# Two token tiles' queries in one projection, by halves of the features

## The chip, the cores and the metric

The kernel runs on one core of one Trainium2 chip. The core has five engines with their own instruction queues: TensorE (matmuls, results go to PSUM), VectorE, ScalarE, GpSimd, and SyncE, which here only issues DMA transfers. Each queue is worked off in its own order, and the engines wait for one another through semaphores. The metric is the device time of one execution in microseconds.

## The reference

Two kinds of layer, A and B, are applied in turn, A B A B, to a residual stream x of 2048 tokens by 512 features. Each adds its result to x after a layer norm. There are 32 heads of 16 features.

```python
x = x + _A_ref(_layernorm(x, axis=-1), A_wq, A_wk, A_wv, A_wo, A_beta)
x = x + _B_ref(_layernorm(x, axis=-1), B_wqkv, B_w_phi, B_wo)
x = x + _A_ref(_layernorm(x, axis=-1), A_wq, A_wk, A_wv, A_wo, A_beta)
x = x + _B_ref(_layernorm(x, axis=-1), B_wqkv, B_w_phi, B_wo)
```

Layer A works on 4 segments of 512 tokens. Within a segment it is causal attention; beside it a memory M, z of the earlier segments is read with phi of the queries and added with a gate.

```python
phi = lambda t: jnp.where(t > 0, t + 1.0, jnp.exp(t))
for s in range(N):
    logits = jnp.einsum('bhqd,bhkd->bhqk', qs, ks) * scale + mask
    p = _softmax(logits, axis=-1)
    a_dot = jnp.einsum('bhqk,bhkd->bhqd', p, vs)
    pq = phi(qs)
    num = jnp.einsum('bhld,bhde->bhle', pq, M)
    den = jnp.einsum('bhld,bhd->bhl', pq, z)[..., None] + 1e-06
    o = g * (num / den) + (1.0 - g) * a_dot
    pk = phi(ks)
    M = M + jnp.einsum('bhld,bhle->bhde', pk, vs)
    z = z + jnp.einsum('bhld->bhd', pk)
```

Layer B is linear attention over all 2048 tokens with softmax features of q and k. The change touches layer A alone, and within it the queries.

## The kernel before

The residual stream X stays in SBUF as 16 token tiles of 128. A segment of layer A, and a chunk of layer B, is four token tiles.

**Layer A's projections** (`a_proj`). The normalized rows of a segment come transposed into `xA`, features on the partitions. For each token tile the kernel projects keys, queries and values. The queries come out with features on the partitions: `fm_mms` makes 16 matmuls for one token tile, four groups g of 128 features by four slices dt of the contraction, each with a 128 x 128 block of `WA_q` as the weights and the tile's 128 tokens as the moving columns. The 16 fill one PSUM bank of 512 columns, ordered by group and then by token. One copy (`q.copy`, on ScalarE or VectorE) takes the bank to `QT`, a buffer for two token tiles (4 groups x 256 tokens), into the tile's 128 columns of each group. In segments 1 to 3 phi of the queries follows, one token tile at a time: an exponential on ScalarE (`phiq.exp`, L944) from `QT` into the buffer `phi`, max(q + 1, 1) on VectorE (`phiq.lin`, L945) into `PhiQ`, and the smaller of the two on VectorE (`phiq.min`, L946). In segment 0 the memory is empty and no phi of the queries is needed. The first two token tiles of segment 0 are projected in a direct form (`by_pe`), with their transposes on TensorE. Keys and values (`WA_k`, `WA_v`) go by `proj_heads`, with tokens on the partitions and 256 columns to a matmul. Keys are then transposed by DMA (`kT.dma`).

**Scores** (`a_att`). A segment has 18 pairs of score tiles, each a PE operation of 8 to 28 matmuls of 32 contraction rows over `QT` and `K`, and two exponentials of 128 x 1024 on ScalarE (L1089) into `PT`. The diagonal blocks are masked on GpSimd and VectorE (L1095, L1098). The products with the values follow on TensorE (rows `PS<-VT,PT` and `PS<-VT,D`), then a reciprocal and a normalization on VectorE (L1123, L1124). A score operation waits for the parts of `QT` that it reads; a part is one token tile.

**The memory read** (`a_mem`) waits for `PhiQ`, and its parts are token tiles too.

**The order of the work** is written out. The program first makes a list of some 3,400 operations, each with the engines that can do it. `replay` then puts them into the queues in the order of the table `ORDER`; `ENGINE` has a letter for each operation that more than one engine can do; `SLOTS` chooses the buffer of each tile; `AFTER` adds waits of one operation for another. A negative entry of ORDER stands for idle matmuls: -1 - 16 n - b puts n matmuls of 240 columns into a corner of PSUM bank b, whose results nobody reads (L1417). The waits themselves follow from what each operation reads and writes.

**The loads** (`setup`, `late_loads`) of X and of the weights stand in the queues of SyncE and ScalarE among the DMA transposes, in the places that ORDER gives them. X comes as four tiles of 128 rows and three loads of 512 rows (segments 1 to 3); VectorE takes statistics of these rows (`stats`, L786) in `ln`.

Of the kernel before, what the change touches and what calls it, by code (L numbers as in the profile page):

```python
# [7 lines left out]
ACT = mybir.ActivationFunctionType  # L8
# [516 lines left out]
class Kernel:  # L525
# [134 lines left out]
    def gen(self):  # L660
        return self.PS.tile(self.genkind)
# [213 lines left out]
    def a_proj(self, s, xnT, pris, by_pe=()):  # L875

        self.P.tag = (self.L, "aproj%d" % s)
        R, P = self.R, self.P
        K, VT = self.p_K.tile(), self.p_VT.tile()
        seg = dict(K=K, VT=VT, KP=[self.p_KP.tile() for _ in range(4)], QT=[self.p_QT.tile() for _ in range(2)])  # L880
        if s >= 1:
            seg["PhiQ"] = self.p_PhiQ.tile()
        if s <= 2:
# [578 lines left out]
```

## Time and profile before

| | before |
|---|---|
| median of 3 runs | 451.51 us |
| lowest, highest | 451.43, 451.68 us |
| the profiled execution's own time | 453.82 us |
| its span, first to last instruction | 452.0 us |
| TensorE busy | 435.1 us (96%) |
| VectorE busy | 417.2 us (92%) |
| ScalarE busy | 412.0 us (91%) |
| GpSimd busy | 258.0 us (57%) |
| mean granted TensorE clock | 0.992 |

PE is TensorE's matmuls, PEld its weight loads, DVE VectorE, ACT ScalarE, POOL GpSimd, SP SyncE. A busy TensorE counts each matmul to the modelled end of its result, so it isn't TensorE at its peak. A row of the timeline has the start, the time, the engine, the line and the operation, out<-in with the shapes, the number of instructions, and in brackets how long the engine was idle before it and what ended that. A row of the windows has a stretch, its length, and for each engine the busy time and the number of instructions; PEclk is the granted clock as a share of full speed, then come the DMA engines' share and GB/s. A row of the groups has the total busy time and the mean in ns, and then the idle time before.

### The profile page before, as it was taken

The numbers are of one execution on the slowest core, as the hardware profiler recorded it, in microseconds if no ns is written. First come the engines' busy times: TensorE is split into PE (matmuls) and PEld (weight loads), VectorE is DVE, ScalarE is ACT, GpSimd is POOL, SyncE is SP. The second block draws the span as 40 slices with busy tenths as digits, with TensorE's granted clock in tenths as the row PEclk, the third lists the DMA queues.
The fourth block names the chain that finished last, engine by engine and source line by source line (L and its number), as shares of the span: only waits on it lengthen the run. The fifth ranks groups of instructions, "written<-read, shape, count | busy, mean of one in ns | idle before, by whom it ended". The sixth has DMA issues, their size and how long they took to land.

```text
span 452.0 us, 19039 instructions
## 1 busy us (share of the span) xinstructions
PE 435.1 (96%) x8236; PEld 303.9 (67%) x8236; DVE 417.2 (92%) x1043; ACT 412.0 (91%) x633; POOL 258.0 (57%) x429
## 2 busy tenths in 40 slices
PE   7979999999999999999999999999999999999996
PEld 6775767667766665757777666876676765675763
DVE  7978999989999899899999999999998989968996
ACT  4989999999999999897899999999999999999730
POOL 4557578675775587330157677766786677814100
PEclk9998999989999999999999999999999999999999
DMA  8986773516213320522525647256134224032377
GB/s 246 235 131 119 107 143 38 85 35 96 50 27 38 62 39 13 74 46 48 74 56 87 96 64 105 49 86 83 27 38 83 49 51 49 3 73 51 76 132 210
DMA packets 115092, 35.86 MB, mean 79 GB/s; under 512 B 106816, under 2 KB 115008, under 8 KB 115008
## 3 DMA queue, kind: packets, MB, share of 16 engines
q1 hardware_dynamic: 112464, 32.41, 42.3%
q10 hardware_dynamic: 2544, 2.24, 1.7%
q8 instruction: 65, 1.06, 1.0%
q14 instruction: 19, 0.16, 0.1%
HBM read 6.32 MB, written 2.10 MB: 19 GB/s over the span
## 4 chain that ended last, share of the span: by engine, by line
ACT 51%; PE 34%; DVE 9%; DMA 3%; issue 1%; SPq 1%; DVEq 0%
ACT PT L1089 38%; PE PS L505 33%; ACT Ek L1185 5%; DMA X<-in_A_x_dram 3%; ACT phi L944 2%; ACT K L1268 2%; ACT phi L933 1%; DVE Vt L1213 1%; PE PS L586 1%; DVE stats L786 1%; ACT VT L564 1%; DVE KV L1240 1%; DVE Rkv L1242 1%; DVE X L1150 1%; DVE PT L1324 1%
## 5 line engine op out<-in xcount | busy, mean ns | idle before, releaser
L1089 ACT ACTIVATE PT<-PS 128x1024 bf16<-128x1024 f32 x288 | 281.6, 1099 | 5.6 <-PE PS L505 4.8
L1098 POOL TENSOR_SCALAR_AFFINE_SELECT PT<-PT 128x512 bf16<-128x512 bf16 x128 | 80.9, 640 | 45.5 <-DVE D L1095 32.5
L1095 POOL TENSOR_TENSOR D<-PT,modd 128x256 bf16<-128x256 bf16 x118 | 77.7, 670 | 36.3 <-ACT PT L1089 10.3
L505 PEld LDWEIGHTS PS<-VT,PT 128*128 128x128 bf16 x2048 | 74.3, 96 | 16.6 <-DVE O L1124 2.0
L505 PE MATMUL PS<-VT,PT 128*128 128x17 bf16 x2048 | 80.5, 171 | 2.3 <-DVE O L1124 1.6
L505 PE MATMUL PS<-VT,D 128*128 128x17 bf16 x512 | 60.0, 171 | 0.0
L505 PE MATMUL PS<-QT,K 32*128 32x64 bf16 (+2 forms) x2176 | 56.3, 214 | 3.8 <-ACT PT L1089 2.4
L786 DVE BATCH_NORM_STATS2 stats<-X 128x6 f32<-128x512 bf16 x64 | 42.5, 677 | 4.2 <-DMA X<-in_A_x_dram 3.9
L1150 DVE TENSOR_TENSOR X<-X,PS 128x512 bf16<-128x512 bf16 x64 | 42.9, 679 | 3.1 <-PE PS L505 2.9
L505 PEld LDWEIGHTS PS<-QT,K 32*128 32x128 bf16 x2176 | 29.5, 93 | 22.0 <-ACT PT L1089 14.5
L505 PEld LDWEIGHTS PS<-VT,D 128*128 128x128 bf16 x512 | 43.2, 96 | 0.0
L1095 DVE TENSOR_TENSOR D<-PT,modd 128x256 bf16<-128x256 bf16 x138 | 38.2, 302 | 3.5 <-ACT PT L1089 3.0
L1213 DVE TENSOR_TENSOR Vt<-PS,Zk 128x1024 bf16<-128x1024 f32 (+1 forms) x34 | 38.8, 1154 | 1.2 <-PE PS L505 0.6
L1185 ACT ACTIVATE Ek<-PS 128x512 bf16<-128x512 f32 x64 | 38.2, 683 | 1.3 <-PE PS L505 1.3
L505 PE MATMUL PS<-xA,WA_q 128*128 128x128 bf16 x512 | 36.3, 224 | 0.3 <-ACT K L906 0.2
L505 PE MATMUL PS<-WA_v,xA 128*128 128x256 bf16 x256 | 35.6, 276 | 0.0
L505 PE MATMUL PS<-WA_k,xA 128*128 128x256 bf16 x256 | 34.6, 273 | 0.3
L1288 POOL COPY O<-rho 128x512 bf16<-128x512 bf16 x26 | 15.7, 622 | 33.4 <-DVE rho L1281 11.3
L1192 POOL TENSOR_TENSOR Vt<-Ek 128x512 f32<-128x512 bf16 x24 | 27.7, 1156 | 10.6 <-ACT Ek L1185 4.8
L505 PEld LDWEIGHTS PS<-xA,WA_q 128*128 128x128 bf16 x512 | 30.7, 100 | 4.4 <-issue 1.3
L505 PE MATMUL PS<-WA_o,OT 128*128 128x512 bf16 x128 | 33.0, 380 | 0.0
L1124 DVE TENSOR_TENSOR O<-PS,r 128x256 bf16<-128x256 f32 (+1 forms) x72 | 27.4, 384 | 1.1
(162 smaller groups left out, 936.0 us busy)
## 6 DMA issues: line engine op xcount, KB each, us to landing
X<-in_A_x_dram SPq DMA_DIRECT2D x3, 512.0 KB, 8.2
out_dram<-X ACTq DMA_DIRECT2D x9, 128.0 KB, 2.1
EQ<-in_B_wqkv_dram SPq DMA_DIRECT2D x2, 512.0 KB, 7.1
out_dram<-X SPq DMA_DIRECT2D x7, 128.0 KB, 2.3
OT<-O SPq DMA_TRANSPOSE x36, 3.3
WA_o<-in_A_wo_dram SPq DMA_DIRECT2D x1, 512.0 KB, 10.7
WB_v<-in_B_wqkv_dram SPq DMA_DIRECT2D x1, 512.0 KB, 6.3
WB_o<-in_B_wo_dram SPq DMA_DIRECT2D x1, 512.0 KB, 5.4
```

The costliest lines, as they stand in the source:

```text
L505: return e.matmul(o, l, r, start=st, stop=sp, tile_position=(basep(l), basep(o)))
L786: self.dve(lambda e, t=t, src=src: e.bn_stats(self.stats[:, t, :], src()), 0.603, [held() if held else R("X", t)], [R("stats", t)], name=" ...
L944: self.act(lambda e, t3=t3, src=src: e.activation(t3.ap[:].rearrange("p (g c) -> p g c", g=NG), src(), ACT.Exp), 512, [sres], [t3()], name ...
L1089: self.act(lambda e, st=st, pt=pt: e.activation(pt.ap[:].rearrange("p b c -> p (b c)"), self.ps[:, st.slot[0] * 512:st.slot[0] * 512 + 102 ...
L1095: self.either(lambda e, d=d, k=k, pt=pt: e.tensor_tensor(d.ap[:, :, k, :].rearrange("p b (z c) -> p b z c", z=2), self.ends(pt.ap[:, :, 25 ...
L1098: self.pool(lambda e, q=quarters: e.affine_select(q(), q(), [[0, 4], [1, 128]], ALU.is_ge, 0.0, base=0, channel_multiplier=-1), 0.6, [pt() ...
L1124: self.dve(lambda e, r1=r1, view=view, nt=nt, g=g, o=o[ts]: e.tensor_tensor(o.ap[:, 0:nt, g, :].rearrange("p i (h d) -> p i h d", d=DH), v ...
L1150: self.dve(lambda e: e.tensor_tensor(X[:, t, :], X[:, t, :], self.bank(gen), ALU.add), 0.6, [R("X", t), gen()], [R("X", t)], name="resid")
L1185: self.act(lambda e, sgn=sgn, Ek=Ek, gen=gen: e.activation(Ek.ap[:, sgn, :], self.bank(gen), ACT.Exp, scale=1.0 - 2.0 * sgn), 512, [gen()] ...
L1192: self.pool(lambda e, Ek=Ek, sums=sums: e.tensor_tensor(sums(), *(Ek.ap[:].rearrange("p s (h j) -> p s h j", h=H)[:, :, :, 8 * k:8 * k + 8 ...
L1213: self.dve(lambda e, w=w, n=n, Vt=Vt, Zk=Zk, gen2=gen2: e.tensor_tensor(self.signed(Vt)[:, w, :, 0:16], self.bank(gen2).rearrange("p (h d) ...
L1288: P.add(("act", "pool"), {"act": lambda e, dst=dst, src=src: e.activation(dst(), src(), ACT.Copy), "pool": lambda e, dst=dst, src=src: e.t ...
```

## The change

The queries of token tiles 0 and 1, and of 2 and 3, of a segment are projected together, when the odd one is reached. There are two halves h of the features: for each half 8 matmuls (two groups by four slices) of 256 columns, both token tiles at once, into a bank of their own, and a copy of the bank into the half's groups of `QT`. A part of `QT` is now a half of the features for both token tiles; so are the parts of `PhiQ`, the exponential, the linear piece and the minimum. `phiq.lin` can go to VectorE or GpSimd; 11 of 24 are given to VectorE and 13 to GpSimd. The direct tiles of segment 0 stay as they were. `seg["q"]` holds for each token tile the two resources that a score has to wait for, and a score now takes that of its group's half.

Of the 512 matmuls with `WA_q`, 448 of 128 columns give way to 224 of 256. The number of operations is unchanged, and all of them outside the queries keep their number in ORDER. ORDER, ENGINE, SLOTS and AFTER are all new. ORDER has 16 entries of idle matmuls in place of 14, with 79 matmuls in place of 76; AFTER has 171 waits in place of 178. Of the tables the core shows only lines of the new ORDER with idle matmuls in them (-39 and -34: two each; -71: four).

```diff
@@ -31,181 +31,182 @@
...
+    191, 363, 724, 364, 211, 232, 216, 217, 196, 233, 237, 175, 214, -39, 201, 15, 202, 203, 204, 726, 205, 215, 365, 428, 176, 341, 218, 219, -34,
...
+    777, 650, 479, 663, 622, 651, 662, 625, 480, 623, 656, 624, 660, 682, 626, -34, 667, 668, 684, 785, 683, 627, 489, 673, 674, 678, 1116, 669, 814,
+    670, -71, 685, 686, 747, 687, 786, 676, 490, 671, 675, 672, 482, 483, 816, 677, 679, 680, 815, 484, 817, 493, 706, 708, 494, 688, 681, 689, 818,
...
@@ -877,7 +878,7 @@
         self.P.tag = (self.L, "aproj%d" % s)
         R, P = self.R, self.P
         K, VT = self.p_K.tile(), self.p_VT.tile()
-        seg = dict(K=K, VT=VT, KP=[self.p_KP.tile() for _ in range(4)], QT=[self.p_QT.tile() for _ in range(2)])
+        seg = dict(K=K, VT=VT, KP=[self.p_KP.tile() for _ in range(4)], QT=[self.p_QT.tile() for _ in range(2)], q={})
         if s >= 1:
             seg["PhiQ"] = self.p_PhiQ.tile()
         if s <= 2:
@@ -933,17 +934,31 @@
                     self.act(lambda e, t2=t2, src=src: e.activation(heads(t2.ap[:]), src(), ACT.Exp), 512, [gen()], [t2()], name="phik.exp")
                     self.dve(lambda e, kt=kt, dst=dst: e.tensor_scalar(heads(dst()), self.spread(kt), 1.0, 1.0, op0=ALU.add, op1=ALU.max), 0.21, [kt()], [res], port=True, name="phik.lin")
                     self.dve(lambda e, t2=t2, dst=dst: e.tensor_tensor(dst(), dst(), t2.ap[:], ALU.min), 0.334, [res, t2()], [res], port=True, name="phik.min")
-            qt, qs = seg["QT"][tt // 2], slice((tt % 2) * 128, (tt % 2) * 128 + 128)
-            t3 = self.p_phi.tile() if s >= 1 else None
-            gen = self.gen()
-            P.pri = pris[tt]
-            self.steps(self.fm_mms(W["q"], xnT, tt, gen), self.wa("q") + [xnT(tt)], gen, pre=[qt] + ([t3] if s >= 1 else []), n=8, name="q")
-            self.copy(lambda qt=qt, qs=qs: qt.ap[:, :, qs], lambda gen=gen: self.bank(gen).rearrange("p (g c) -> p g c", g=NG), 512, [gen()], [qt(tt % 2)], name="q.copy")
-            if s >= 1:
-                dst, res, src, sres = (lambda sl=sl: seg["PhiQ"].ap[:, :, sl]), seg["PhiQ"](tt), (lambda qt=qt, qs=qs: qt.ap[:, :, qs]), qt(tt % 2)
-                self.act(lambda e, t3=t3, src=src: e.activation(t3.ap[:].rearrange("p (g c) -> p g c", g=NG), src(), ACT.Exp), 512, [sres], [t3()], name="phiq.exp", cost=0.52)
-                self.dve(lambda e, dst=dst, src=src: e.tensor_scalar(dst(), src(), 1.0, 1.0, op0=ALU.add, op1=ALU.max), 0.21, [sres], [res], port=True, name="phiq.lin")
-                self.dve(lambda e, t3=t3, dst=dst: e.tensor_tensor(dst(), dst(), t3.ap[:].rearrange("p (g c) -> p g c", g=NG), ALU.min), 0.334, [res, t3()], [res], port=True, name="phiq.min")
+            if direct:
+                qt, qs = seg["QT"][tt // 2], slice((tt % 2) * 128, (tt % 2) * 128 + 128)
+                gen = self.gen()
+                P.pri = pris[tt]
+                self.steps(self.fm_mms(W["q"], xnT, tt, gen), self.wa("q") + [xnT(tt)], gen, pre=[qt], n=8, name="q")
+                self.copy(lambda qt=qt, qs=qs: qt.ap[:, :, qs], lambda gen=gen: self.bank(gen).rearrange("p (g c) -> p g c", g=NG), 512, [gen()], [qt(tt % 2)], name="q.copy")
+                seg["q"][tt] = [qt(tt % 2)] * 2
+            elif tt % 2:
+                qt, sl = seg["QT"][tt // 2], slice((tt - 1) * 128, (tt + 1) * 128)
+                P.pri = pris[tt - 1]
+                for h in range(2):
+                    t3 = self.p_phi.tile() if s >= 1 else None
+                    gen = self.gen()
+                    mms = [(lambda g=g, dt=dt, h=h, gen=gen, tt=tt: (self.bank(gen)[:, (g - 2 * h) * 256:(g - 2 * h + 1) * 256], W["q"][:, dt, g * 128:(g + 1) * 128],
+                                                                     self.xtiles(xnT)[:, tt - 1:tt + 1, dt, 0:128], dt == 0, dt == 3), 256) for g in (2 * h, 2 * h + 1) for dt in range(4)]
+                    self.steps(mms, self.wa("q") + [xnT(tt - 1), xnT(tt)], gen, pre=[qt] + ([t3] if s >= 1 else []), n=4, name="q")
+                    self.copy(lambda qt=qt, h=h: qt.ap[:, 2 * h:2 * h + 2, :].rearrange("p g c -> p (g c)"), lambda gen=gen: self.bank(gen), 512, [gen()], [qt(("g", h))], name="q.copy")
+                    for i in (tt - 1, tt):
+                        seg["q"].setdefault(i, []).append(qt(("g", h)))
+                    if s >= 1:
+                        dst, res, src, sres = (lambda sl=sl, h=h: seg["PhiQ"].ap[:, 2 * h:2 * h + 2, sl]), seg["PhiQ"]((tt // 2, h)), (lambda qt=qt, h=h: qt.ap[:, 2 * h:2 * h + 2, :]), qt(("g", h))
+                        two = lambda t3=t3: t3.ap[:].rearrange("p (g c) -> p g c", g=2)
+                        self.act(lambda e, t3=t3, src=src, two=two: e.activation(two(), src(), ACT.Exp), 512, [sres], [t3()], name="phiq.exp", cost=0.48)
+                        self.either(lambda e, dst=dst, src=src: e.tensor_scalar(dst(), src(), 1.0, 1.0, op0=ALU.add, op1=ALU.max), 0.21, 0.6, [sres], [res], name="phiq.lin")
+                        self.dve(lambda e, two=two, dst=dst: e.tensor_tensor(dst(), dst(), two(), ALU.min), 0.334, [res, t3()], [res], port=True, name="phiq.min")
             P.pri = pris[tt] + (2.0 if by_pe else 0.0)
             gen = self.proj_heads(W["v"], self.wa("v"), xnT, tt, pre=[VT], name="v")
             self.copy(lambda tt=tt: VT.ap[:, tt, :, 0:16].rearrange("p (a b) d -> p b a d", b=2), lambda gen=gen: halves(gen), 512, [gen()], [VT(tt)], name="v.copy")
@@ -983,14 +998,14 @@
         AM, r2 = self.p_AM.tile(), self.p_r2.tile()
         gen = self.gen()
         self.pe([(lambda i=i, g=g: (self.bank(gen)[:, i * 32 + 8 * g:i * 32 + 8 * g + 8], PhiQ.ap[:, g, i * 128:(i + 1) * 128], MSb.ap[:, g, :, 16], True, True), 8)
-                 for i in range(4) for g in range(NG)], [PhiQ(i) for i in range(4)] + [MSb(1)], [gen()], pre=[r2], name="den")
+                 for i in range(4) for g in range(NG)], [PhiQ((t, h)) for t in range(2) for h in range(2)] + [MSb(1)], [gen()], pre=[r2], name="den")
         dst = lambda: r2.ap[:].rearrange("p i h -> p (i h)")
         self.dve(lambda e: e.tensor_scalar(dst(), self.bank(gen, 128), DEN_EPS, None, op0=ALU.add), 0.21, [gen()], [r2()], name="den.eps")
         self.dve(lambda e: e.reciprocal(dst(), dst()), 0.87, [r2()], [r2()], name="den.rec")
         for i in range(4):
             g2 = self.gen()
             self.pe([(lambda g=g, i=i, g2=g2: (self.bank(g2)[:, g * 128:(g + 1) * 128], PhiQ.ap[:, g, i * 128:(i + 1) * 128], MSb.ap[:, g, :, 0:16], True, True), 128)
-                     for g in range(NG)], [PhiQ(i), MSb(0), r2()], [g2()], pre=[AM], name="am")
+                     for g in range(NG)], [PhiQ((i // 2, h)) for h in range(2)] + [MSb(0), r2()], [g2()], pre=[AM], name="am")
             self.dve(lambda e, i=i, g2=g2: e.tensor_tensor(AM.ap[:, i, :].rearrange("p (h d) -> p h d", h=H), self.bank(g2).rearrange("p (h d) -> p h d", h=H),
                                                      r2.ap[:, i, :, None].to_broadcast([128, H, DH]), ALU.mult), 0.6, [g2(), r2()], [AM(i)], name="am.mul")
         return AM
@@ -1075,11 +1090,11 @@
                 g = item[1]
                 if item[0] == "S":
                     par, j, qs = item[2:]
-                    reads += [K((par, j)), K((par, j, 1)), K(("both", j))] + [QT[i // 2](i % 2) for i in qs]
+                    reads += [K((par, j)), K((par, j, 1)), K(("both", j))] + [seg["q"][i][g // 2] for i in qs]
                     put(lambda a, par=par, g=g, j=j: strip(a, par, g, j), item, qs[0] * 128, off, 128 * len(qs))
                 else:
                     i = item[2]
-                    reads += [K((1, i)), K((0, i)), K((1, i, 1)), K(("both", i)), seg["KP"][i](), QT[i // 2](i % 2)]
+                    reads += [K((1, i)), K((0, i)), K((1, i, 1)), K(("both", i)), seg["KP"][i](), seg["q"][i][g // 2]]
                     put(lambda a, g=g, i=i: both(a, g, i), item, i * 128, off, 64)
                     for par in range(2):
                         put(lambda a, par=par, g=g, i=i: strip(a, par, g, i), item, i * 128 + 64, 6 + off // 4 if par else off + 1, 64)
```

More of the change, by code (lines that the diff above doesn't have):

```diff
@@ L33 @@
 ORDER = (
[135 rows of a table removed]
[135 rows of a table added]
 )
 AFTER = (
[17 rows of a table removed]
[17 rows of a table added]
 )
 ENGINE = (
[L190 to L193 removed]
+    "aaddaadapaapaddpadpdpdpadddapdpdppdddpdddddddpppppppppddddddpdddpdpapapdpdpaddpdpdpdaddddadadppppppppppdppppppdddddddddddppdpppppdddddddddpa"
@@ L194 @@
+    "dddapdddpdpdddddddpdppdpppppdddddpppdddddpppddppppddppdpppdpdpddddpdddpdddpddddaddddddddppddppppdddpdddpddddpddpddpddpddpdddppppddddddaappap"
+    "apppaaaaaaaddaaapaapdaapaadadaadddaapppdppddppddpddpddpdpddpddpdppdddapdpadapapadadapdpddapdapppppppdppppppppdddddpddddpdpdpppppdppppdddpapd"
+    "aadapdddpdpaaapaddpaddppppppddppppdddddddpddddpppddddpdppppppdddddpapddddaddddpdddpdddpdpdppppppddddddddddppddddddppppdppdddpddpdddpdddaapap"
+    "aappasaaasassssaasasasda"
 )
 SLOTS = (
-    "00030010120110132260011103001801000001202301111210320045011217910320011231210231010121381000002231041000313211356100223010113079011212200370"
@@ L205 @@
-    "10100021530211471012032106120010351000213212011001121304801001110379011102332211301002001302901220157011013280231123013121049012130214010110"
-    "10003510201972100532012002210100141031100310225601020123801011023201030002101220120012140110133750100000112223369011131201300130131482102100"
-    "01206012202501000122207901130202010110102323010213001451020002010147015010202230007003120110024531112260010220033106112403101202001313101213"
-    "451549310411036102378203442050157"
+    "00110010020101301800112103010312012203210690111310102033410110057102011030022160122130002139201022318010103120341000011213057013021222093021"
@@ new lines @@
+    "12701452030210820101102031031013210201179011300201121004012000025210100220301102201701133101015201114612030001120820013901010303002170112110"
+    "00304610210231032350110020290113010130102031003110315010017821203010129201211003512012002000810120311792012001121201000000310500113021340102"
+    "13680210021010203311150101012210210100100134301322167100011230890123120001610020213334010211057011121302010394121100086201001512201234020790"
+    "10124120000100101231001223035011013368011012310103240100320279012121030135010300222100142013101232000011022123203067012111224011000310812101"
@@ new lines @@
+    "90010203001350123226701201228012310001020101000211034110210113030112310501002030032033302363110231425220001231100120033011200230101312112322"
+    "02013008101100123130013012110102240112032003112010030760122311151001001212230101224910111311300670120301012010110100111031010025812020112001"
+    "03112201671002001520231010203080200130100111000110010233038100012211131113101011003002101200214901031560201178120201000203102001113011013010"
+    "21123327801000111230324501001323069011211002000011401201318301123000325710031110161002341210218901010111030013012120337410005612013012010011"
@@ L209 @@
+    "12412011380223079011120110102011038100022013240100002137501110102016901210120032301032211149011210326801001022520100134121079010010236101310"
+    "00247010128920000012110223200014501100120331002060131001131701012132301030021123120910100030311216401300322112185013101103120011000179210031"
+    "12230102003450131103003681011200130700101202010006100743021010122210040200001100513122120273020113212060231400003000109213261103450030114207"
+    "315044523364002320026367805112501"
 )
```

12 lines of the change are left out of this document (removed), and 301 rows, old and new, of tables (AFTER, ORDER).

## The prediction

> **What bounds the kernel now.** I read the page's head first, then busy time over nine stretches, cut where the chain of waits passes from TensorE to ScalarE or back.
>
> ```profile
> span 452.0 us, 19039 instructions
> PE 435.1 (96%) x8236; PEld 303.9 (67%) x8236; DVE 417.2 (92%) x1043; ACT 412.0 (91%) x633; POOL 258.0 (57%) x429
> ACT 51%; PE 34%; DVE 9%; DMA 3%; issue 1%; SPq 1%; DVEq 0%
> ```
>
> ```profile
> core 0: us, PE busy (x) PEld busy (x) DVE busy (x) ACT busy (x) POOL busy (x), PEclk, DMA share, GB/s
> 0.00:41.69 41.69, 36.28 (x651) 29.23 (x652) 34.25 (x111) 32.33 (x47) 24.00 (x53) 0.96 0.92 194
> 41.69:97.70 56.01, 53.40 (x1157) 38.10 (x1158) 55.01 (x146) 55.98 (x71) 39.74 (x68) 1.00 0.52 81
> 97.70:109.82 12.12, 12.03 (x259) 9.72 (x260) 10.74 (x32) 11.01 (x15) 5.69 (x11) 0.86 0.56 89
> 109.82:167.05 57.23, 55.95 (x1192) 37.96 (x1193) 53.58 (x140) 57.15 (x76) 39.12 (x60) 1.00 0.27 44
> 167.05:254.28 87.23, 86.35 (x1454) 59.86 (x1448) 82.77 (x195) 79.19 (x149) 37.76 (x60) 1.00 0.38 61
> 254.28:318.17 63.89, 63.57 (x1259) 44.41 (x1258) 61.18 (x159) 63.81 (x87) 45.48 (x74) 1.00 0.49 76
> 335.81:383.24 47.43, 46.66 (x944) 31.16 (x944) 43.84 (x106) 47.42 (x65) 33.83 (x53) 1.00 0.41 64
> 383.24:452.00 68.76, 64.40 (x899) 41.50 (x899) 58.73 (x117) 47.52 (x113) 18.56 (x33) 1.00 0.42 90
> ```
>
> ScalarE has no gap in 41.69 to 97.70, 109.82 to 167.05, 254.28 to 318.17 and 335.81 to 383.24 (55.98 of 56.01, and so on): there only less ScalarE work shortens the span. The start, the turn of the layers (167.05 to 254.28) and the tail go by TensorE and what feeds it. So I looked for ScalarE's gaps, and for what stood behind the largest.
>
> ```profile
> 28.17 1.98 ACT L1089 ACTIVATE PT<-PS 128x1024 bf16<-128x1024 f32 x2
> 32.30 1.94 ACT L1089 ACTIVATE PT<-PS 128x1024 bf16<-128x1024 f32 x2 [1.65 <-PE PS L505]
> 35.76 1.94 ACT L1089 ACTIVATE PT<-PS 128x1024 bf16<-128x1024 f32 x2 [0.52 <-PE PS L505]
> 38.60 0.60 ACT L933 ACTIVATE phi<-PS 128x512 bf16<-128x512 f32 x1 [0.41 <-DVE ktok L564]
> 93.80 6.60 ACT L1089 ACTIVATE PT<-PS 128x1024 bf16<-128x1024 f32 x7
> 101.37 1.94 ACT L1089 ACTIVATE PT<-PS 128x1024 bf16<-128x1024 f32 x2 [0.97 <-PE PS L505]
> ```
>
> ```profile
> 19.63 0.40 DVE L802 TENSOR_SCALAR xn<-X,mv,rstd 128x512 bf16<-128x512 bf16 x1
> 20.29 2.58 SPq L570 DMA_TRANSPOSE xA<-xn  x1
> 22.91 0.58 SPq L572 DMA_DIRECT2D X<-in_A_x_dram  x1
> 28.94 0.69 DVE L786 BATCH_NORM_STATS2 stats<-X 128x6 f32<-128x512 bf16 x1 [2.06 <-DMA X<-in_A_x_dram]
> 30.83 0.23 PE L505 MATMUL PS<-VT,PT 128*128 128x17 bf16 x3 [1.60 <-DVE O L1124]
> ```
>
> The rows of X for the third segment are asked for at 22.91, behind a transpose that holds SP's queue 2.58, and land six microseconds later. VectorE is in order, so it stands 2.06 at their statistics, with the normalization of the first probability products behind it; TensorE waits 1.60 for that, ScalarE 1.65 for TensorE. The third view is the granted clock, in stretches of 3.4:
>
> ```profile
> 26.32:29.74 3.42, 2.62 (x72) 2.24 (x69) 1.35 (x6) 3.42 (x6) 2.40 (x4) 1.00 1.28 149
> 29.74:33.15 3.41, 2.32 (x80) 2.14 (x81) 3.41 (x15) 1.76 (x3) 1.99 (x5) 1.00 0.16 36
> 33.15:36.56 3.41, 3.41 (x31) 2.33 (x29) 2.13 (x8) 2.89 (x5) 2.02 (x5) 0.50 0.69 123
> 94.58:98.00 3.42, 2.88 (x100) 2.31 (x100) 3.35 (x8) 3.42 (x5) 2.90 (x8) 1.00 0.02 5
> 98.00:101.41 3.41, 3.41 (x50) 2.99 (x47) 2.42 (x8) 2.44 (x4) 2.02 (x3) 0.50 0.40 77
> 319.84:323.26 3.42, 3.25 (x130) 2.74 (x127) 3.09 (x8) 3.42 (x5) 1.41 (x2) 1.00 0.02 5
> ```
>
> Twice TensorE runs 3.41 us at half clock, each time right after a stretch in which it was busy only 2.32 or 2.88 of 3.4, with short matmuls (80 and 100 records). ScalarE's gaps of 0.52, 0.41 and 0.97 lie inside or at the end of those two stretches.
>
> **The change, part by part.**
>
> *Matmuls.* 448 matmuls of 128 columns go, 224 of 256 columns come: seven eighths of the 512 of the query projection. Columns, and PSUM written, stay the same; weight loads halve for them.
>
> ```profile
> 26.12 1.06 PE L505 MATMUL PS<-xA,WA_q 128*128 128x128 bf16 x16
> 58.02 1.04 PE L505 MATMUL PS<-WA_v,xA 128*128 128x256 bf16 x8
> L505 PEld LDWEIGHTS PS<-xA,WA_q 128*128 128x128 bf16 x512 | 30.7, 100 | 4.4 <-issue 1.3 <-ACT K L906 0.4 <-ACT QT L564 0.4
> ```
>
> Sixteen of 128 columns take 1.06, eight of 256 take 1.04: what a token tile's queries cost before and after. 28 such groups are replaced: 28 x 0.02 = 0.6 us less TensorE time, of which about eight groups lie in TensorE's own stretches: -0.2. The saved weight loads ran beside the matmuls already (16 loads inside 1.06), so they count nothing; were they not hidden, 224 x 0.06 (30.7 / 512 each) would be 13 us. The Trainium skill (TensorE: Matmul & The Clock Gate, Back-to-back issue gap) gives about 81 ns a matmul at 128 columns and 131 at 512 in a stream of weight loads and matmuls; by it, with an estimated 98 ns at 256 columns, the change would take 448 x 81 - 224 x 98 = 14 us from TensorE. The trace does not agree with it: the two bursts come to 66 ns and 130 ns a matmul with their ends.
>
> *Copies and exponentials.* As many as before, 512 elements each. The exponential of the queries now reads one dense run per partition, not four strips.
>
> ```profile
> L944 ACT ACTIVATE phi<-QT 128x512 bf16<-128x512 bf16 x24 | 15.9, 671 | 0.0
> L933 ACT ACTIVATE phi<-PS 128x512 bf16<-128x512 f32 x20 | 12.5, 633 | 0.5 <-DVE ktok L564 0.4
> L945 DVE TENSOR_SCALAR PhiQ<-QT 128x512 bf16<-128x512 bf16 x24 | 6.9, 298 | 0.0
> L923 POOL COPY KP<-K 128x512 bf16<-128x512 bf16 x23 | 14.1, 615 | 17.0 <-ACT K L906 10.1 <-DVE PhiQ L945 3.1 <-DVE O L1134 2.0
> L1134 POOL TENSOR_TENSOR O<-O,AM 128x512 bf16<-128x512 bf16 x3 | 3.5, 1153 | 0.4 <-DVE mv L787 0.4
> POOL PT L1098 <- DVE D L1095: 32.5, 34, 4.0
> ```
>
> At best it comes down to the neighbouring exponential: 24 x (671 - 633) = 0.9 us; at worst nothing. I take -0.4; most of these lie where ScalarE has no gap.
>
> *The linear half of phi on two engines.* Of its 24 instructions (L945) the new list of engines leaves 11 on VectorE and puts 13 on GpSimd. VectorE is freed of 13 x 0.298 = 3.9 us, GpSimd gets 13 times an operation it has not shown: between 0.615 (its copy of that size, one input) and 1.153 (two inputs); by its one input it is nearer 0.615: 8 us. GpSimd is idle 16.3 of 56.0 in the second stretch, so this is hidden unless it delays the masks queued behind it; GpSimd waits for VectorE's masks in 34 places already. VectorE's gain counts nothing where ScalarE sets the pace. I put +0.5 for this and the other new waits (below).
>
> *The pair.* The queries of an even tile now wait for the odd tile's transpose. From the second segment on one transpose brings both, so this costs nothing; in the first segment they come singly, but there the fourth tile's queries already ran ahead of the third's, so only two matmul groups move, by under 1.06 us, beside ScalarE's exponentials. A score now waits for one half of the features instead of a tile, which is never later than both halves; the memory read (L988 and on) waits for both halves, half a segment ahead of its use. Residues: inside the +0.5.
>
> *The order.* I counted the new list against the old: the matmul columns ahead of each pair of scores, idle matmuls aside, are never more than 1.1 us apart, and what stands ahead of each exponential on ScalarE no more than 1.1 either, but at the turn of the layers (1.4 less): a close variant, not another plan. No term is made of that. Three differences bear on the gaps.
>
> First, VectorE has 0.44 us more to do ahead of the statistics at which it waits (the same count, by mean durations), and the first normalization of probability products stands ahead of them, not behind. The key copy that holds SP's queue ahead of the transpose at 20.29 comes 0.7 earlier, so that transpose waits for its rows alone (19.63 + 0.40 = 20.03): X is asked for some 0.26 earlier. One load of X moves from the first 8 us to behind the first key transpose, and the output weights of the first layer behind the second load; the queues are otherwise passed by the same transposes. VectorE should stand 2.06 - 0.44 - 0.26 = 1.4. Bounds: ScalarE's gap of 1.65 stays, or goes. I take -0.7.
>
> Second, the list has four idle matmuls between the scores of the exponentials at 28.17 and 32.30, where it had none, just where TensorE was thin ahead of the first half clock. Each costs
>
> ```profile
> 209.39 0.51 PE PS L1417 x5
> ```
>
> a tenth of a microsecond, in a wait of 1.60. With 0.7 less waiting and 0.4 of idle matmuls the stretch's 2.32 would come to the whole 3.41. Bounds: 0 to -0.93 (the gaps 0.52 and 0.41); I take -0.5, since it is not known what the clock follows.
>
> Third, six idle matmuls stand in the second segment between its 25th and 29th exponential, where there was none. The segment's 36th ends where the row at 93.80 does, so these are eight to twelve of 0.94 earlier, 89 to 93: just ahead of the stretch from 94.58, not in it. Bounds: 0 to -0.97; I take half, -0.5.
>
> The Trainium skill (TensorE: Matmul & The Clock Gate, Why this matters for your kernels) has the clock fall after a gap of some 3 us without matmuls. Here it fell with no gap over 1.60, so the trace sets the limit higher; by that rule the last two terms would be nothing, and the sum -0.8.
>
> Sum: -0.2 - 0.4 - 0.7 - 0.5 - 0.5 + 0.5 = -1.8 us. The profiled execution took 453.82 in all with a span of 452.0; the runs' median is 451.51, so the profiled one is 2.3 slower. I carry the difference over: 451.5 - 1.8 = **449.7 us**, -0.4%. This kernel's measurement can't tell less than 0.2%, 0.9 us, from no change.
>
> **The rivals.**
>
> *Nothing reaches the end.* The load lands as late, the half clocks come back one window on, and the rest is under 0.9. For it: the columns are the same, so is nearly all of ScalarE's work, and what the clock follows is guessed from two cases. -0.2 - 0.4 + 0.3: 451.2.
>
> *GpSimd becomes late.* Place: the 13 linear halves in GpSimd's queue ahead of the masks that the diagonal's probability products wait for, in ScalarE's stretches. Price: at 1.153 each is 0.85 later than VectorE's 0.298; were a third of the 13 to reach a score, 4 x 0.85 = 3.4, less the 0.6 of matmuls and exponentials: 454.3. It decides once GpSimd has no slack in front of a mask; against it stand the 34 waits of GpSimd for VectorE, 32.5 us.
>
> *A half clock somewhere else.* The stretch at 319.84 shows such short matmuls (130) and full clock; another order can fall under what it held to. One more costs up to 3.41 / 2 = 1.7; with half the gains of the start that is -0.2 - 0.4 - 0.6 + 0.5 + 1.7 = +1.0: 452.5.
>
> *TensorE does get shorter*, because weight loads count after all where other matmuls stand between. Of the 13 us, eight groups of 28 lie in TensorE's own stretches: 3.7 on top of the forecast, 446.0. Against it: the bursts. (It is what the Trainium skill's figure, above, comes to here.)
>
> **How the numbers follow.** Forecast 0.47, nothing 0.22, GpSimd 0.14, another half clock 0.12, TensorE 0.05. The range: all gains of the forecast (-0.2 - 0.9 - 1.65 - 0.93 - 0.97 = -4.65) give 446.9, hardly together, so 447.2 below; above 453.0, which takes in the other half clock and leaves out most of GpSimd. The forecast's own range is 447.5 to 450.6. Faster by over 0.2%: the forecast, TensorE, and a little of nothing: 0.54; within: 0.23; slower: 0.23.
>
> **What would show it.** Queries: eight matmuls of 256 columns in about 1.04, and the same sum of matmul columns. L944's successor between 633 and 671. VectorE's wait for X under 2.06, ScalarE's largest gap after 12 us under 1.65. Full clock in the first 45 us and from 90 to 110. The linear half on GpSimd near 0.6, and TensorE not waiting for GpSimd more than now. Wrong it would be if the half clocks are there as before or elsewhere, if VectorE stands as long for X, or if ScalarE shows gaps behind GpSimd in its four stretches.

## The result, and the profile after

The change makes the kernel slower: 464.9 us in the median of 4 runs (463.17 to 466.17) against 451.6 (451.43 to 452.23) of the kernel before beside it; the ratio is 1.029, with a 95% interval of 1.025 to 1.033. The forecast was 449.7, the range ended at 453.0. The profiled execution took 463.17 us with a span of 461.4.

The head of the page of the changed kernel: span, busy time by engine, and the chain of waits by engine.

```profile
span 461.4 us, 18525 instructions
PE 428.4 (93%) x7949; PEld 297.7 (65%) x8015; DVE 422.6 (92%) x1034; ACT 412.4 (89%) x632; POOL 281.7 (61%) x439
ACT 46%; PE 26%; DVE 16%; POOL 9%; issue 2%; DMA 1%; ACTq 0%; DVEq 0%; POOLq 0%
```

ScalarE has the work that it had (412.0 before), TensorE has less (435.1 before). VectorE is busy 5.4 us longer (417.2 before), although 13 linear halves have left it. GpSimd has 23.7 us more, where 8 were forecast, and stands in the chain with 9% of the span, where before it did not appear.

The groups of the changed kernel: the queries' exponential, the linear half on GpSimd and on VectorE, the minimum that follows it, and the matmuls with their weight loads.

```profile
L959 ACT ACTIVATE phi<-QT 128x512 bf16<-128x512 bf16 x24 | 15.7, 670 | 0.0
L960 POOL TENSOR_SCALAR PhiQ<-QT 128x512 bf16<-128x512 bf16 x13 | 25.4, 1953 | 5.1 <-DVE mv L788 1.3 <-DVE xn L803 1.2 <-ACT QT L565 1.0
L960 DVE TENSOR_SCALAR PhiQ<-QT 128x512 bf16<-128x512 bf16 x11 | 3.6, 330 | 0.0
L961 DVE TENSOR_TENSOR PhiQ<-PhiQ,phi 128x512 bf16<-128x512 bf16 x24 | 13.5, 568 | 5.8 <-POOL PhiQ L960 5.8
L506 PE MATMUL PS<-xA,WA_q 128*128 128x256 bf16 (+1 forms) x288 | 33.4, 261 | 2.5 <-DVE PhiQ L961 2.3
L506 PEld LDWEIGHTS PS<-xA,WA_q 128*128 128x128 bf16 x288 | 23.8, 98 | 8.3 <-DVE PhiQ L961 2.8 <-DVE O L1139 1.1 <-issue 0.4
```

On GpSimd the linear half takes **1.953 us**, six times VectorE's 0.330, and well above the 0.615 to 1.153 that the prediction allowed it. VectorE waits 5.8 us for it, and its minimum, 0.415 before, takes 0.568 in the mean.

How such a delay reaches the end is seen in the chain of waits over ten microseconds of the second segment (start, time, what):

```profile
82.68 0.21 DVE D L1110
82.89 0.08 issue
82.97 1.94 POOL PhiQ L960
84.91 0.02 issue
84.93 1.37 DVE PhiQ L961
86.30 0.60 DVE VT L565
86.91 0.61 DVE ktok L565
87.51 0.02 issue
87.54 0.60 ACT phi L934
88.13 0.49 ACT Ek L1200
88.62 1.83 ACT PT L1104 x2
```

The minimum is the next instruction in VectorE's queue. VectorE executes in order, so the copies of the values and of the keys stand behind it; ScalarE, in order too, waits 1.04 us for the keys before it can go on to the exponentials. The wait is not the whole delay. In the timeline the minimum begins after 0.30 us of idle time and then takes 1.37, beside a product that GpSimd starts right behind its linear half:

```profile
84.93 1.37 DVE L961 TENSOR_TENSOR PhiQ<-PhiQ,phi 128x512 bf16<-128x512 bf16 x1 [0.30 <-POOL PhiQ L960]
84.87 1.15 POOL L1207 TENSOR_TENSOR Vt<-Ek 128x512 f32<-128x512 bf16 x1
```

The median of the 24 minima is 0.420. Three take 1.30 to 1.37, each beside this product, and each ends 0.28 us after it. So the linear half on GpSimd also brings the minimum and the product together; a cheaper instruction in its place (below) takes this apart from the wait in part. The waits of the whole execution (waiting <- waited for: sum, times, longest):

```profile
DVE PhiQ L961 <- POOL PhiQ L960: 5.8, 6, 1.8
PE PS L506 <- DVE PhiQ L961: 3.9, 5, 1.3
PE PS L506 <- POOL PT L1113: 2.6, 4, 1.2
POOL PT L1113 <- DVE D L1110: 15.1, 24, 2.1
ACT PT L1104 <- PE PS L506: 6.6, 10, 1.2
ACT phi L934 <- DVE ktok L565: 3.0, 2, 1.9
```

TensorE now waits behind the minimum and, less, for GpSimd's masks; neither stood among its waits before.

### The profile page after: what moved, and what is told of

It reads as the page before. It is cut to its first block, busy times and chain, and to the rows that moved or that the text cites. A ratio compares the mean times of both kernels' runs of the same rounds, so it can differ in the third digit from the quotient of the medians.

```text
span 461.4 us, 18525 instructions
## 1 busy us (share of the span) xinstructions
PE 428.4 (93%) x7949; PEld 297.7 (65%) x8015; DVE 422.6 (92%) x1034; ACT 412.4 (89%) x632; POOL 281.7 (61%) x439
## 4 chain that ended last, share of the span: by engine, by line
ACT 46%; PE 26%; DVE 16%; POOL 9%; issue 2%; DMA 1%; ACTq 0%; DVEq 0%; POOLq 0%
ACT PT L1104 34%; PE PS L506 25%; POOL PhiQ L960 4%; ACT Ek L1200 4%; POOL PT L1113 2%; POOL D L1110 2%; ACT K L1283 2%; DVE Vt L1228 2%; DVE stats L787 1%; DMA beta<-in_A_beta_dram 1%; DVE D L1110 1%; ACT phi L934 1%; DVE ktok L565 1%; ACT EQ L1283 1%; PE PS L587 1%
## 5 line engine op out<-in xcount | busy, mean ns | idle before, releaser
L1113 POOL TENSOR_SCALAR_AFFINE_SELECT PT<-PT 128x512 bf16<-128x512 bf16 x128 | 81.0, 646 | 28.2 <-DVE D L1110 15.1
L506 PEld LDWEIGHTS PS<-VT,PT 128*128 128x128 bf16 x2048 | 74.6, 96 | 23.7 <-POOL PT L1113 4.3
L1110 DVE TENSOR_TENSOR D<-PT,modd 128x256 bf16<-128x256 bf16 x137 | 40.0, 311 | 0.6 <-ACT PT L1104 0.5
L1303 POOL COPY O<-rho 128x512 bf16<-128x512 bf16 x29 | 17.1, 615 | 36.8 <-DVE xn L803 19.6
L506 PE MATMUL PS<-WA_k,xA 128*128 128x256 bf16 x256 | 37.0, 276 | 1.7 <-DVE PhiQ L961 1.6
L1207 POOL TENSOR_TENSOR Vt<-Ek 128x512 f32<-128x512 bf16 x24 | 28.0, 1166 | 12.8 <-ACT Ek L1200 9.6
L506 PE MATMUL PS<-xA,WA_q 128*128 128x256 bf16 (+1 forms) x288 | 33.4, 261 | 2.5 <-DVE PhiQ L961 2.3
L506 PE MATMUL PS<-WA_o,OT 128*128 128x512 bf16 x112 | 29.4, 380 | 1.8 <-issue 0.6
L506 PEld LDWEIGHTS PS<-xA,WA_q 128*128 128x128 bf16 x288 | 23.8, 98 | 8.3 <-DVE PhiQ L961 2.8
```

Of the source, the lines that this page charges most:

```text
L506: return e.matmul(o, l, r, start=st, stop=sp, tile_position=(basep(l), basep(o)))
L1110: self.either(lambda e, d=d, k=k, pt=pt: e.tensor_tensor(d.ap[:, :, k, :].rearrange("p b (z c) -> p b z c", z=2), self.ends(pt.ap[:, :, 25 ...
L1113: self.pool(lambda e, q=quarters: e.affine_select(q(), q(), [[0, 4], [1, 128]], ALU.is_ge, 0.0, base=0, channel_multiplier=-1), 0.6, [pt() ...
L1207: self.pool(lambda e, Ek=Ek, sums=sums: e.tensor_tensor(sums(), *(Ek.ap[:].rearrange("p s (h j) -> p s h j", h=H)[:, :, :, 8 * k:8 * k + 8 ...
L1303: P.add(("act", "pool"), {"act": lambda e, dst=dst, src=src: e.activation(dst(), src(), ACT.Copy), "pool": lambda e, dst=dst, src=src: e.t ...
```

## The experiments

### All linear halves on VectorE, twice

Everything else stays as changed.

```diff
             op.on = {"a": "act", "d": "dve", "p": "pool", "s": "sp"}[c]
+        for op in ops:
+            if op.name == "phiq.lin":
+                op.on = "dve"
```

> The changed kernel with all 24 linear halves of the queries' phi on VectorE, everything else (256-column matmuls, halves, order, idle matmuls) as changed. Theory P (price: the 13 linear halves at 1.95 us on GpSimd are the whole loss): the 9 of them that stand in the chain go, VectorE gets 13 x 0.30 = 3.9 us more, and what is left is the forecast without its last term: 449 to 452 us. Theory O (the new order or the pairing of tiles costs it, GpSimd only shows it): 460 to 465 us. Half and half would come out near 457.

> All 24 linear halves on VectorE once more, beside the split one on the same chip: 449.1 to 450.0 us, 0.9926 to 0.9968 of before.

449.53 us, 0.9947 of before (0.9926 to 0.9968), and again 450.27, 0.9968 (0.9943 to 0.9994). So 13 instructions on another engine are the whole loss, 15 us; without them the change gains 0.3 to 0.5%, and no kernel or variant here that computes the whole has a lower median. Its timeline at the same place as the chain above:

```profile
79.64 0.28 DVE L963 TENSOR_SCALAR PhiQ<-QT 128x512 bf16<-128x512 bf16 x1
80.18 0.42 DVE L964 TENSOR_TENSOR PhiQ<-PhiQ,phi 128x512 bf16<-128x512 bf16 x1
80.85 0.42 DVE L964 TENSOR_TENSOR PhiQ<-PhiQ,phi 128x512 bf16<-128x512 bf16 x1
80.97 1.30 POOL L1210 TENSOR_TENSOR Vt<-Ek 128x512 f32<-128x512 bf16 x1 [2.21 <-ACT Ek L1203]
81.18 0.69 DVE L568 CAST VT<-PS 128x512 bf16<-128x512 f32 x1
81.78 0.68 DVE L568 CAST ktok<-PS 128x512 bf16<-128x512 f32 x1
82.56 0.65 ACT L937 ACTIVATE phi<-PS 128x512 bf16<-128x512 f32 x1
```

VectorE and ScalarE go on without a wait here. Against this trace the changed kernel loses 12.8 us between its first exponential of the scores and its last, nearly all in 14 places of 0.3 to 1.8 us, spread over both passes of layer A (behind exponentials 18, 36, 38, 56, 94, 96, 162, 164, 176, 178, 200, 202, 204 and 256 of 288, by their starts). Its groups show how little idle time is left ahead of the exponentials (1.2 us, against 7.3 in the changed kernel), and what the 24 linear halves cost VectorE; the 24 minima come to 0.431 each in this trace, 3.3 us less in all than in the changed kernel:

```profile
L1107 ACT ACTIVATE PT<-PS 128x1024 bf16<-128x1024 f32 x288 | 281.0, 1091 | 1.2 <-PE PS L509 0.7
L963 DVE TENSOR_SCALAR PhiQ<-QT 128x512 bf16<-128x512 bf16 x24 | 8.4, 350 | 0.2
```

### The kernel before with 13 linear halves on GpSimd

```diff
+        for j, op in enumerate(op for op in ops if op.name == "phiq.lin"):
+            if j in (0, 1, 2, 3, 4, 7, 9, 12, 13, 15, 16, 19, 23):
+                op.eng, op.emit = ("pool",), {"pool": op.emit["dve"]}
```

> The kernel before with 13 of its 24 linear halves moved to GpSimd, the same places by number as in the changed kernel, at the positions in the order that VectorE had for them; nothing else is touched. Theory P: each becomes 1.95 instead of 0.30 us and a good part of 13 x 1.65 = 21 us comes through: 460 to 470 us. Theory O: the old order carries it, 451 to 455 us.

469.63 us, 1.039 of before (1.034 to 1.044). The old order and the old tiles carry the instruction no better: +17.6 us. With the runs above, that rules the new order out as the cause.

### What the instruction costs by itself

The kernel before, and behind its end single instructions in `X`'s place, four or more of each, such as

```diff
+        for _ in range(4):
+            self.pool(lambda e: e.tensor_scalar(D, S, 1.0, 1.0, op0=ALU.add, op1=ALU.max), 0.6, [end], [end], name="trial")
```

> The kernel before, followed, when all its work is done, by single instructions of 128x512 bf16 on GpSimd with VectorE at rest, then with VectorE at work; the time is longer by these (some 75 us) and says nothing. Theory P1 (the price belongs to the instruction: addition and maximum in one): about 1.9 us with VectorE at rest, one operation or a copy about 0.6, addition of two tensors 1.15. Theory P2 (the price comes from the port shared with VectorE): 0.6 to 1.2 with VectorE at rest and about 1.9 beside it. VectorE's own: 0.30 and 0.41 alone, more beside GpSimd if the two get in each other's way.

Its groups, with VectorE at rest in the first seven: on GpSimd L1425 is addition and maximum, L1427 addition alone, L1429 maximum alone, L1431 multiplication and addition, L1433 addition of two tensors, L1435 a copy, L1437 addition and maximum of half the size; L1441 is VectorE's own addition and maximum. In L1447 and L1449 the two engines do addition and maximum beside each other; in L1458 VectorE does it beside GpSimd's copies.

```profile
L1425 POOL TENSOR_SCALAR X<-X 128x512 bf16<-128x512 bf16 x4 | 7.7, 1925 | 0.3
L1427 POOL TENSOR_SCALAR X<-X 128x512 bf16<-128x512 bf16 x4 | 6.0, 1489 | 0.3
L1429 POOL TENSOR_SCALAR X<-X 128x512 bf16<-128x512 bf16 x4 | 5.9, 1485 | 0.3
L1431 POOL TENSOR_SCALAR X<-X 128x512 bf16<-128x512 bf16 x4 | 2.5, 618 | 0.3
L1433 POOL TENSOR_TENSOR X<-X 128x512 bf16<-128x512 bf16 x4 | 4.6, 1148 | 0.3
L1435 POOL COPY X<-X 128x512 bf16<-128x512 bf16 x4 | 2.4, 612 | 0.2
L1437 POOL TENSOR_SCALAR X<-X 128x256 bf16<-128x256 bf16 x4 | 4.3, 1069 | 0.3
L1441 DVE TENSOR_SCALAR X<-X 128x512 bf16<-128x512 bf16 x4 | 1.2, 294 | 50.8 <-POOL X L1439 50.7
L1447 POOL TENSOR_SCALAR X<-X 128x512 bf16<-128x512 bf16 x6 | 11.9, 1986 | 3.6 <-DVE X L1443 3.2
L1449 DVE TENSOR_SCALAR X<-X 128x512 bf16<-128x512 bf16 x8 | 3.3, 415 | 0.3
L1458 DVE TENSOR_SCALAR X<-X 128x512 bf16<-128x512 bf16 x8 | 4.4, 547 | 5.6 <-POOL X L1452 5.3
```

The price belongs to the instruction: 1.925 us with VectorE at rest, 1.986 beside it. One addition or maximum alone was expected at 0.6 and took 1.49. The rule of one input is no guide: with one input GpSimd takes 0.612 for a copy, 0.618 for multiplication and addition, 1.49 for an addition or a maximum alone and 1.93 for both. The Trainium skill (GPSIMD Engine Reference, Engine selection) calls one-input work on GpSimd roughly line-rate. Here five instructions with one input and 512 elements take 0.612 to 1.925, so the rule can hold for the copy and for multiplication with addition at most, not for the other three.

### Three other prices in the same 13 places

Each variant puts another instruction into GpSimd's 13 places of the changed kernel and leaves the linear half, or a part of it, out there: a copy (neither addition nor maximum), the queries added to themselves, the maximum alone.

```diff
...
+                        op.emit = {"dve": op.emit["dve"], "pool": lambda e, dst=dst, src=src: e.tensor_copy(dst(), src())}
...
```

> The changed kernel where GpSimd's 13 linear halves only copy the queries (the addition and the maximum are left out; 128x512 bf16 as before): the instruction that my low bound of 0.615 us priced. Theory P: with that price the forecast holds, 449 to 452 us. Theory L (the place, not the price: a linear half in GpSimd's queue is late at any price): above 456 us.

> The changed kernel where GpSimd's 13 linear halves are an addition of the queries to themselves (the linear half itself is left out): an instruction with the price of 1.15 us that my high bound had. My rival's sum was 454.3 (a third of the 13 reach a score, 0.85 each). In proportion between 0.615 us (448.95) and 1.953 us (464.9) it would be 455.3. If GpSimd has slack that only a price above 1.15 uses up: 449 to 451.

> The changed kernel where GpSimd's 13 linear halves do the maximum alone (the addition is left out), the instruction that took 1.485 us by itself. With 0.615 the time was 448.95, with 1.04 451.36, with 1.953 464.9. If the loss grows evenly from the second to the third, 14.8 us per us of price: 458. If GpSimd's slack ends between 1.49 and 1.95: under 454. If it ends before: 458 to 461.

| on GpSimd, 13 times | us each | median us | of before (95%) |
|---|---|---|---|
| copy | 0.615 | 448.95 | 0.9934 (0.9900 to 0.9967) |
| queries plus themselves | 1.04 | 451.36 | 0.9994 (0.9963 to 1.0026) |
| maximum alone | 1.52 | 456.81 | 1.0115 (1.0066 to 1.0164) |
| addition and maximum | 1.95 | 464.9 | 1.0289 (1.0254 to 1.0325) |

(The addition of one tensor to itself took 1.04, not the expected 1.15.) The places are good: at the price of a copy the change does what was forecast. From there each step adds 5.5 to 6.2 us to GpSimd, and 2.4, 5.4 and 8.1 us to the kernel: more and more of it comes through. In the first step VectorE hardly waits yet for GpSimd's part (0.2 us in the whole trace), but its minima take 0.520 us in the mean, against 0.435 with the copy: 2.0 us in all, and one of them is 1.37 beside GpSimd's product. So the slow minimum may be most of the first step, and the wait comes in with the dearer instructions (3.3 and 5.8 us). Part of the 8.1 can be half clocks: the granted clock was 0.989 to 0.996 in the four runs with addition and maximum, and 1.0 in three of the four with the maximum alone. The 456.81 lies between the two cases expected for it, under 454 where slack ends late and 458 for an even loss. The four points show no threshold; that slack ends at one place after the other fits them, and was not tried by itself.

### A cheap instruction that keeps the computation whole

GpSimd multiplies by one and adds one; VectorE's minimum becomes the maximum with one and the minimum.

```diff
+                        op.emit = {"dve": op.emit["dve"], "pool": lambda e, dst=dst, src=src: e.tensor_scalar(dst(), src(), 1.0, 1.0, op0=ALU.mult, op1=ALU.add)}
+                        self.dve(lambda e, two=two, dst=dst, op=op: e.scalar_tensor_tensor(dst(), dst(), 1.0, two(), op0=ALU.max, op1=ALU.min) if op.on == "pool" else
+                                 e.tensor_tensor(dst(), dst(), two(), ALU.min), 0.334, [res, t3()], [res], port=True, name="phiq.min")
```

> The changed kernel, all 13 GpSimd places kept, with the whole computation: GpSimd does queries times one plus one (the pair of operations that took 0.618 us by itself), and VectorE's minimum that follows becomes a maximum with one and the minimum in a single instruction. Theory P (the price of addition and maximum in one is the whole loss, the places are good): 448.7 to 449.7 us, as with the copy (448.95) and with all on VectorE (449.53). If the longer VectorE instruction counts (13 of at most 0.8 us instead of 0.43): up to 452.

450.84 us, 0.9986 (0.9956 to 1.0016): 14 us of the 15 are back, with GpSimd's part at 0.617 each (the median of its tile's rows), but nothing is won over VectorE doing it all (450.27 beside it). The time is above the 449.7 of theory P and inside what was expected if the longer VectorE instruction counts: that takes 0.684 (median of 13) where the minimum takes 0.419.

### What the rest of the change does

Three runs take parts from the version with all linear halves on VectorE, or give one to the kernel before. First, two matmuls of 128 columns for each of 256:

```diff
...
-                                                                     self.xtiles(xnT)[:, tt - 1:tt + 1, dt, 0:128], dt == 0, dt == 3), 256) for g in (2 * h, 2 * h + 1) for dt in range(4)]
+                                                                     self.xcol(xnT, dt, tt - 1 + i), dt == 0, dt == 3), 128) for g in (2 * h, 2 * h + 1) for i in range(2) for dt in range(4)]
...
```

> As the run with all linear halves on VectorE (449.53 us, 0.9947 of before), but each matmul of 256 columns of the queries is two of 128 columns again, in the same place: pairs, halves, order and idle matmuls stay. Forecast's step (16 of 128 columns take 1.06 us, 8 of 256 take 1.04, and only eight groups of 28 lie where TensorE sets the pace): 0.2 us longer, 449.5 to 450.2. Rival 'TensorE does get shorter' (saved weight loads count): 3.7 us longer, about 453.

452.70 us, 1.0011 (0.9983 to 1.0040): 2 to 3 us longer. Of the runs at a granted clock of 0.998 or more, so apart from any half clock, 8 of it have a median of 452.0, 23 of the version with 256 columns 450.0. These 23 were measured on other chips; six such runs on the same chip, of the version with 256 columns without ten idle matmuls (below), have 450.4. So 1.6 to 2.0 us belong to the wide matmuls. ScalarE is idle 4.1 us ahead of the exponentials of the scores, against 1.2 with 256 columns; gaps of 0.86 and 0.43 stand where the other has none and 0.19:

```profile
244.94 1.94 ACT L1107 ACTIVATE PT<-PS 128x1024 bf16<-128x1024 f32 x2 [0.86 <-PE PS L509]
307.26 1.94 ACT L1107 ACTIVATE PT<-PS 128x1024 bf16<-128x1024 f32 x2 [0.43 <-PE PS L509]
```

Second, the version with all on VectorE without the ten idle matmuls near 30 and 93 us (the entries -39, -34, -34 and -71 of the order); third, the kernel before with ten idle matmuls put at these places of its own order.

> As the run with all linear halves on VectorE (449.53 us, granted clock 0.998 to 1.0 in every run), without the ten idle matmuls that the new order has near 30 us and near 93 us. Forecast's step (they keep the clock up): half-clock stretches come back, mean clock 0.996 or less in most runs, and 0.5 to 1.0 us longer: 450.0 to 450.6. Rival (the clock is steady for another reason, the nearer arrival of work, say): clock 0.998 to 1.0 and 449.2 to 449.8.

> The kernel before with ten idle matmuls added at the same places of the work (two ahead of and two behind the last probability products ahead of the score whose exponential stood at 32.30 us; two and four about the products near 89 to 93 us), nothing else. The kernel before ran at a mean clock of 0.985 to 1.0, 452.0 us in the median, 450.9 where its clock was 1.0. Forecast's step: clock 0.998 to 1.0 in most runs, 450.5 to 451.3. Rival (idle matmuls do nothing for the clock): clock 0.996 in most, 451.8 to 452.6.

Without them: 450.62 us, 0.9968 (0.9942 to 0.9994), and 6 of 12 runs at 0.998 or more, against 23 of 24 with them. The trace without them has a half clock at 95.08 us, behind a stretch in which TensorE is busy 2.65 of 3.42, and none near 30; its other one, at 9.74, is not at a place where any were taken out. Added to the kernel before: 453.26 us, 1.0004 (0.9970 to 1.0037), above both ranges that were expected, and 5 of 12 runs, which can't be told from its own 20 of 80. In the new order they keep the clock, but the time that they are worth can't be told from the noise (450.62 against 449.53 and 450.27); in the old order they are not enough. The windows of the kernel before with ten more show it for the first place: ahead of the half clock TensorE is busy 1.96 of 3.42 us.

```profile
27.12:30.54 3.42, 1.96 (x60) 1.58 (x57) 2.21 (x8) 3.42 (x6) 2.53 (x5) 1.00 1.39 117
30.54:33.95 3.41, 2.81 (x72) 2.29 (x73) 2.13 (x9) 0.56 (x2) 1.92 (x5) 0.50 0.27 52
33.95:37.36 3.41, 3.41 (x33) 2.81 (x32) 2.41 (x8) 2.75 (x4) 0.94 (x3) 0.50 0.41 79
```

## Why the prediction was wrong

**The step that failed** is the last term, +0.5 "for this and the other new waits", and in it the bounds of the linear half on GpSimd: "between 0.615 (its copy of that size, one input) and 1.153 (two inputs); by its one input it is nearer 0.615". The term is some +15 us (464.9 against 449.5 and 450.3), because the linear half takes 1.953 on GpSimd. Neither end was a bound: the nearest rows were other operations, and the operation decides. With the price that I took, the copy's, the kernel measured 448.95, inside the forecast's own range.

**The rival of a late GpSimd** had the mechanism and its price as a function of the duration, but not the duration: at 1.153 it put 3.4 us on the path; measured at 1.04 is 2.4 over the copy. Its route was only part of it. I had put it in the masks behind the linear half; the chain shows the minimum ahead of the copies in VectorE's queue, and TensorE waits more for that (3.9 us) than for the masks (2.6). That the minimum itself becomes slow beside GpSimd's product was in no rival. The 34 waits of GpSimd for VectorE's masks, which I counted as slack (32.5 us), shrank to 24 with 15.1 and were no protection for what waits for GpSimd itself.

**Matmuls, -0.2:** mis-sized; -1.6 to -2.0 by the run with 128 columns. The bursts are as I read them (16 of 128 columns in 1.06, 8 of 256 in 1.04, in both traces again), so the sum over bursts left something out. The rival in which TensorE gets shorter had the direction and about twice the size (-3.7 on top), with a chance of 0.05. What makes 128 columns cost more here is not shown.

**The dense read, -0.4:** nothing; L959 takes 670 ns, L944 took 671.

**The load of X, -0.7:** the wait is as forecast, the gain is not all kept. In the version with all on VectorE the waits are:

```profile
DVE stats L790 <- DMA X<-in_A_x_dram: 1.3, 1, 1.3
ACT rd L715 <- DMA beta<-in_A_beta_dram: 2.0, 1, 2.0
```

1.3 us after 2.06, where I had 1.4; but ScalarE now waits 2.0 for beta at the start (0.57 before), and the first exponential of the scores starts at 13.05 instead of 11.93. I looked at the loads behind 20 us and not at those ahead of it. That the wait for beta makes the exponential late is not shown: the chain of waits of that trace runs through TensorE there. At a clock of 0.998 or more the version with 128 columns is 0.8 us longer than the kernel before measured beside it (452.0 against 451.2, 8 runs each), and 1.2 longer than all such runs of the kernel before (450.8): order, pairs and halves, the start among them, cost about that much; how it divides was not tried.

**The two half clocks, -0.5 each:** about right in sum. The kernel before has a median of 450.8 in 20 runs at a granted clock of 0.998 or more, 451.8 in 38 at 0.994 to 0.996 and 454.2 in 22 at 0.992 or less; the version with all on VectorE is at 0.998 or more in 23 of 24. The median of all 80 runs is 451.9, so a full clock is worth 1.2 us. The forecast took both half clocks of the profiled execution (granted clock 0.992) off the median of the runs; only 22 of the 80 are that low, so that the two sizes agree is in part luck.

So the sum without its last term, -2.3, was met (-1.6 and -2.5 by the two medians beside those of before), but with other terms: -1.6 to -2.0 for the wide matmuls, -1.2 for the clock, +0.8 to +1.2 for the rest. That it came out is luck.

## What to carry to other kernels

Before an operation is moved to another engine, measure that operation there, with its very pair of functions: a row of the same shape and number of inputs is no bound. Ask of a moved instruction not only what is queued behind it on its new engine but where in the old engine's queue its consumer stands: an in-order queue passes the whole delay on to what has nothing to do with it. And compare a list of work with and without a change of size inside the real mix, since the isolated bursts gave a forecast of about a tenth of what the mix showed.

## What the runs showed that I had not expected

**The price of GpSimd's tensor-with-scalar instruction goes by its functions:** 0.618 us for multiplication and addition, 1.49 for one addition or one maximum, 1.925 for both; half the elements take 1.069, so by an estimate from these two sizes some 0.21 is fixed and the rest per element.

**VectorE slows beside GpSimd:** its addition and maximum take 0.294 alone, 0.415 beside GpSimd's, 0.547 beside GpSimd's copies. These are means of two kinds: beside GpSimd's, five of eight still take 0.294 and three 0.58 to 0.66. In the changed kernel three minima took 1.30 to 1.37 instead of 0.42 beside a GpSimd product.

**The half clock goes with how much of the array TensorE used, in fixed stretches of 3.41 us.** In the 12 traces of these kernels I counted the columns of the matmuls that start in each stretch (from 4 us to 430, those on 32 rows as a quarter). All 12 stretches that a half clock follows have at most 3,270 columns, 11 of them at most 2,990; the fewest in a stretch that none follows are 2,940. Busy time doesn't tell them apart. In the changed kernel the first of these stretches has 3,360 columns and a full clock follows it; the second has 2,490, and the clock halves:

```profile
35.79:39.20 3.41, 2.12 (x21) 1.11 (x22) 2.52 (x7) 1.66 (x2) 2.79 (x3) 1.00 0.54 96
59.68:63.09 3.41, 2.32 (x86) 2.06 (x88) 2.50 (x9) 2.60 (x5) 3.41 (x5) 1.00 0.20 39
```

This is a count over traces; no run changed the columns of a stretch and nothing else. The stretches lie differently in each execution, so that a thin place can be hit in some runs and not in others, which fits the spread of the kernel before in part: at a granted clock of 0.998 or more its runs still lie between 449.7 and 452.1. The Trainium skill (TensorE: Matmul & The Clock Gate, Part 1: The HAM clock gate) has windows of 3413 ns that don't start with the kernel, and the clock falling after an idle one. The traces agree with the first (stretches of 3.41 us that begin at another time in each); for the second they show that a window busy 2.88 us can be followed by a half clock as well.
